# Running the body of a fused attention and token-mixing kernel as 64-row products

## The chip, the cores and the metric

The kernel runs on one core of one Trainium2 chip. The time is that of one execution on the device, in microseconds (us). TensorE (PE) multiplies and writes to the PSUM banks; VectorE (DVE) and ScalarE (ACT) read PSUM, GpSimd (POOL) does not in this kernel; SyncE (SP) mostly issues DMAs.

## The reference

Two layers follow each other, for each of 8 batches, with a sequence of 3200 rows:

```python
B, S, D = 8, 3200, 256;  d_qk = d_hyper = 64
scores = (1.0 / S) * z @ z.T             # z: S x 64
attn   = np.maximum(scores, 0.0) ** 2
x      = u * (attn @ v)                  # u, v: S x 256
wq, wk = x @ w_q, x @ w_k                # S x 64
mixed  = (1.0 / np.sqrt(64)) * (wq @ wk.T) @ x
out    = np.maximum(mixed, 0.0) @ w_out
```

The second layer has no nonlinearity between its two products, so the kernel forms `wk.T @ x` (64 x 256, the "heads") first and multiplies `wq` by that (the "mix").

## The kernel before

**Tiling.** A batch's 3200 rows are 25 row tiles of 128, in seven groups: six of 512 rows and a last one of 128 (`LASTG`). A score tile is one row tile against one group. Since the scores are symmetric, a tile that lies near the diagonal is computed once and turned by a DMA transpose for its mirror image (`is_turned`, tiles `tt` and `ttl`). All tiles to be scored stand in one list, `tiles`, and are taken in pairs.

**A score pair** (`scores`, L209). `z` is held transposed and twice, in the upper and the lower 64 partitions (`zT2`), so the two products of a pair use 64 rows of the array each and go into the two banks of one PSUM slot. There are three such slots (`ps_tile`, pool `pps`). The slot is emptied with a ReLU (`first_stage`, L232 on DVE, L228 on ACT) into `g`, and `second_stage` squares it (L247 on POOL, L245 on ACT) into the fp16 tile `at`.

**The second product** (`second_product`, L287). For each of a group's four blocks of 128 rows and each of 25 row tiles, one product with all 128 rows and 256 columns adds to an accumulator. A group's accumulators fill two banks, `acc0` (blocks 0 and 1) and `acc1` (blocks 2 and 3). When a half is complete, `gate` (L313) multiplies it by `u` on DVE and writes `x`; `turn_x` transposes `x` by DMA.

**The second layer.** `projections` (L335) gives queries and keys, two products of 128 rows; `turn_keys` transposes the keys by DMA; `double_keys_queries` copies queries by DMA (L359) and keys on POOL (L360) into the other half; `heads` (L366) adds up `wk.T @ x` over the groups; `mix` (L414, 64-row products) and `proj` (L439, 128-row products) follow, with evictions on ACT (L426, L463) and a DMA of the result. The last group's mix and projection are squeezed into a slot of another step (`side_mix`, `side_proj`).

**The order** is written by hand as phases (the `while groups` loop). A phase scores up to six tiles, stages them, and then issues some 24 second products; a mix or a set of keys and heads goes into a phase when `mix_due` or `key_due` says so. Loads and turns are hung on phase numbers (`due`). A head (`first_pair`, `turn_first`) and a tail (`last_gram`, `last_heads`, and the last mixes and projections) are written out one by one.

Of the kernel before, what the change touches and what calls it, by code (L numbers as in the profile page):

```python
# [16 lines left out]
def kernel(  # L17
# [17 lines left out]
    ND = D // P  # L35
    W = 512
    widths = [512] * 6 + [128]
    starts = [sum(widths[:i]) for i in range(len(widths))]
    NG = len(widths)
    assert sum(widths) == S and dqk == 64 and dh == 64 and ND == 2  # L40

    LAG = 2
# [7 lines left out]
    NAT = 14  # L50

# [8 lines left out]
    pg = ctx.enter_context(tc.tile_pool(name="pg", bufs=8))  # L60
# [3 lines left out]
    pq = ctx.enter_context(tc.tile_pool(name="pq", bufs=9))  # L64
    prt = ctx.enter_context(tc.tile_pool(name="prt", bufs=3))
    pps = ctx.enter_context(tc.tile_pool(name="pps", bufs=3, space=bass.MemoryType.PSUM))
# [5 lines left out]
    def acc_tile(half, name, dtype=FP32):  # L72
        n = W if dtype == FP32 else 2 * W
        return pacc.tile([P, n], dtype, tag=f"acc{half}", name=name)
# [5 lines left out]
    def rows(t, b):  # L80
        return t[b].rearrange("(p n) d -> p n d", n=NT)

# [28 lines left out]
    def turn_first(c):  # L111
        n0, nn = ZCH[c]
        if c < 2:
            tp = acc_tile(c, "ztp", FP16)
# [12 lines left out]

    def load_z(b):
# [18 lines left out]

    wq32 = consts.tile([P, ND, dh], FP32, tag="wq32", name="wq32")
    wk32 = consts.tile([P, ND, dh], FP32, tag="wk32", name="wk32")
    wqk = consts.tile([P, ND, 2, dh], FP16, tag="wqk", name="wqk")  # L150
    wq2 = consts.tile([P, ND, 2, dh], FP16, tag="wq2", name="wq2")
# [4 lines left out]
    def load_weights():  # L156
        wo32[0] = px.tile([P, ND, D], FP32, tag="x_sb", name="wo32")
        nc.sync.dma_start(out=wq32[:], in_=moe_w_q.rearrange("(c p) h -> p c h", p=P))
        nc.sync.dma_start(out=wk32[:], in_=moe_w_k.rearrange("(c p) h -> p c h", p=P))
        nc.sync.dma_start(out=wo32[0][:], in_=moe_w_out.rearrange("(c p) e -> p c e", p=P))  # L160

    def cast_weights():
        nc.gpsimd.tensor_copy(out=wqk[:, :, 0, :], in_=wq32[:])
        nc.gpsimd.tensor_copy(out=wqk[:, :, 1, :], in_=wk32[:])
        for half in range(2):
            nc.gpsimd.tensor_copy(out=wq2[:, :, half, :], in_=wq32[:])
            nc.gpsimd.tensor_copy(out=wk2[:, :, half, :], in_=wk32[:])
        nc.gpsimd.tensor_copy(out=wo[:], in_=wo32[0][:])

    LASTG = NG - 1

# [5 lines left out]

    def rows_of(gi):
        return [starts[gi] // P + n for n in range(widths[gi] // P)]
# [16 lines left out]
    NTILE = len(tiles)  # L200
    made, turned = {}, {}

    def scores(p0):
        pair = tiles[p0 : p0 + 2]
        sc = ps_tile("sc")
        for h, (b, gi, ti) in enumerate(pair):
            gs, gw = starts[gi], widths[gi]
            half = h * dqk
            nc.tensor.matmul(  # L209
                out=sc[:, h, 0:gw],  # L210
                lhsT=zT[b][half : half + dqk, ts(ti, P)],
                rhs=zT[b][half : half + dqk, ds(gs, gw)],
# [5 lines left out]
    def pieces(p0):  # L218
        ws = [widths[gi] for _, gi, _ in tiles[p0 : p0 + 2]]
# [4 lines left out]
    def first_stage(p0, sc, on_act):  # L224
        g = pg.tile([P, 2, W], FP32, tag="g", name="g")
        for hs, w in pieces(p0):
# [11 lines left out]
    def second_stage(p0, g, on_act):  # L238
        at = pat.tile([P, 2 * W], FP16, tag="at", name="at")
        at0 = 0  # L240
        for hs, w in pieces(p0):
# [8 lines left out]
        for tile_ in tiles[p0 : p0 + 2]:  # L250
# [8 lines left out]
        for b, gi, gj, n0, nn, c0, c1 in blocks:  # L259
# [8 lines left out]
    accs = {}  # L268

    def weights(b, gi, ti, j):  # L270

# [6 lines left out]
    def second_product(b, gi, rows_, first, last):  # L278

        nj = widths[gi] // P  # L280
        halves = range((nj + 1) // 2)
        if first:
            for half in halves:
                accs[half] = acc_tile(half, f"acc{half}")

        def one(ti, j):
            nc.tensor.matmul(  # L287
                out=accs[j // 2][:, ds((j % 2) * D, D)],
                lhsT=weights(b, gi, ti, j),
                rhs=vs[b][:, ti, :],  # L290
                start=(first and ti == rows_[0] and j % 2 == 0),
                stop=(last and ti == rows_[-1] and (j % 2 == 1 or j == nj - 1)),
            )

        todo = []
        if last:
            for half in halves:
                for ti in rows_:
                    for j in range(2 * half, min(2 * half + 2, nj)):
                        todo.append(lambda ti=ti, j=j: one(ti, j))  # L300
                run = todo.pop()
                todo.append(lambda run=run, half=half: (run(), gate(b, gi, half)))
        else:
            for ti in rows_:
                for j in range(nj):
                    todo.append(lambda ti=ti, j=j: one(ti, j))
        return todo

    def gate(b, gi, half):
        if half == 0:  # L310
            xs[b, gi] = px.tile([P, 4, D], FP16, tag="x_sb", name="x_sb")
        n = min(2, widths[gi] // P - 2 * half)
        nc.vector.tensor_mul(  # L313
            out=xs[b, gi][:, 2 * half : 2 * half + n, :].rearrange("p n d -> p (n d)"),
            in0=accs[half][:, 0 : n * D],
            in1=us[b, gi][:, 2 * half : 2 * half + n, :].rearrange("p n d -> p (n d)"),
        )
        if 2 * half + n == widths[gi] // P:
            us.pop((b, gi))
            turn_x(b, gi)  # L320

    def turn_x(b, gi):
        nn = widths[gi] // P
        xTs[b, gi] = pxt.tile([P, 4, ND, P], FP16, tag="xT_sb", name="xT_sb")
        nc.sync.dma_start_transpose(
            out=xTs[b, gi][:, 0:nn, :, :].rearrange("p n a s -> p (n a) s"),
            in_=xs[b, gi][:, 0:nn, :].rearrange("p n d -> p (n d)"),
        )


    def projections(b, gi, w, out, start=True):

        gw = widths[gi]
        for ac in range(ND):
            nc.tensor.matmul(  # L335
                out=out,
                lhsT=w[:, ac, :, :].rearrange("p t h -> p (t h)"),
                rhs=xTs[b, gi][:, 0 : gw // P, ac, :],
                start=(start and ac == 0),
                stop=(ac == ND - 1),  # L340
            )

    def projections_out(b, gi, out):
        gw = widths[gi]
        qks[b, gi] = pq.tile([P, W], FP16, tag="qk", name="qk")
        nc.scalar.copy(out=qks[b, gi][:, 0:gw], in_=out)  # L346

    def turn_keys(b, gi):
        gw = widths[gi]
        ks[b, gi] = pk.tile([P, 4, 2, dh], FP16, tag="kx", name="kx")  # L350
        nc.sync.dma_start_transpose(
            out=ks[b, gi][:, 0 : gw // P, :, :].rearrange("p n a h -> p n (a h)"),
            in_=qks[b, gi][:, 0:gw],
        )

    def double_keys_queries(b, gi):
        gw = widths[gi]
        nn = gw // P
        nc.sync.dma_start(out=qks[b, gi][dh:P, 0:gw], in_=qks[b, gi][0:dh, 0:gw])  # L359
        nc.gpsimd.tensor_copy(out=ks[b, gi][:, 0:nn, 0, :], in_=ks[b, gi][:, 0:nn, 1, :])  # L360

    def heads(b, gis, ps, stop=True):

        parts = [(gi, n) for gi in gis for n in range(widths[gi] // P)]
        for gi, n in parts:
            nc.tensor.matmul(  # L366
                out=ps[:, 1, 0:D],
                lhsT=ks[b, gi][:, n, :, :].rearrange("p a h -> p (a h)"),
                rhs=xs[b, gi][:, n, :],
                start=((gi, n) == parts[0]),  # L370
                stop=(stop and (gi, n) == parts[-1]),
            )

    def heads_out(b, gis, ps):
        if gis[0] == 0:
            hacc[b] = psml.tile([P, D], FP32, tag="ha", name="ha")
            nc.vector.tensor_copy(out=hacc[b][:], in_=ps[:, 1, 0:D])
        elif gis[-1] < LASTG:
            nc.vector.tensor_add(out=hacc[b][:], in0=hacc[b][:], in1=ps[:, 1, 0:D])  # L379
        else:  # L380
            heads_done(b, ps[:, 1, 0:D])

    def heads_done(b, part):
        hss[b] = psml.tile([P, D], FP16, tag="hs", name="hs")
        nc.vector.tensor_add(out=hss[b][:], in0=hacc.pop(b)[:], in1=part)  # L385

    def last_gram(b, gi, ps):
        nj = widths[gi] // P
        for n in range(nj):
            for cc in range(ND):  # L390
                nc.tensor.matmul(
                    out=ps[:, ds(cc * D, D)],
                    lhsT=xs[b, gi][:, n, ds(cc * P, P)],
                    rhs=xs[b, gi][:, n, :],
                    start=(gi < LASTG and n == 0 and cc == 0),
# [402 lines left out]
```

## Time and profile before

| | |
|---|---|
| three timed runs | 820.94, 819.31, 819.62 us; median 819.62 |
| span of the profiled execution | 815.5 us |
| TensorE's mean granted clock | 0.997 |
| PE / DVE / ACT / POOL busy | 791.9 / 490.1 / 476.7 / 487.0 us |
| second products (L287) | 5000 instructions, 67% of the chain that ended last |
| scores (L209) | 920 instructions, 13% of the chain |
| DMA, mean of the span | 176 GB/s |

The profile is of one execution, and its span is from the first to the last instruction; the time of an execution is some 4 us more. Matmuls are pipelined and the ends of their records are modelled, so the pitch of a stream of products is read from start to start, and not from a record's duration.

### The profile page before, as it was taken

Reading aid. Unit: us, or ns where it says so; the run is one execution under the profiler, and the core shown is the slowest. Engines: PE = TensorE matmul, PEld = TensorE weight load, DVE = VectorE, ACT = ScalarE, POOL = GpSimd, SP = SyncE. Lnnn points to the kernel's source line nnn. Section 1 sums busy time; section 2 is a strip of 40 time slices with the busy share of each in tenths; the row PEclk is TensorE's granted clock in tenths of the full one; section 3 lists DMA queues with packets and bytes.
Section 4 is the critical chain, followed back from the end, with each engine's and each line's share of the span. In section 5 each row is a group of like instructions: output and inputs, shape, how many; then the busy total and the mean of one; then the engine's idle time right before and its main releaser. Section 6 shows DMA issues by size and latency. Waiting matters only on the chain.

```text
span 815.5 us, 16776 instructions
## 1 busy us (share of the span) xinstructions
PE 791.9 (97%) x6778; PEld 585.5 (72%) x6778; DVE 490.1 (60%) x515; ACT 476.7 (58%) x529; POOL 487.0 (60%) x352
## 2 busy tenths in 40 slices
PE   6899999999999999999999999999999989999995
PEld 3677777777777777777777777777777757767773
DVE  3756566556675566755666556755665546655524
ACT  4655556555665566656665656755675645565545
POOL 5976677555775647654576446854676446665510
PEclk9999999999999999999999999999999999999999
DMA  5999999997999959997999969999899995778436
GB/s 108 212 170 189 133 182 174 198 196 143 181 182 205 216 116 203 165 236 162 194 169 198 205 145 181 188 201 172 189 167 171 192 215 129 158 151 174 113 100 239
DMA packets 331389, 143.20 MB, mean 176 GB/s; under 512 B 307440, under 2 KB 313392, under 8 KB 331312
## 3 DMA queue, kind: packets, MB, share of 16 engines
q1 hardware_dynamic: 302752, 125.70, 74.7%
q0 software_dynamic: 28272, 15.98, 18.4%
q8 instruction: 53, 0.87, 0.5%
q10 hardware_dynamic: 288, 0.46, 0.2%
q14 instruction: 24, 0.20, 0.1%
HBM read 59.38 MB, written 26.21 MB: 105 GB/s over the span
## 4 chain that ended last, share of the span: by engine, by line
PE 93%; DMA 2%; issue 2%; DVE 1%; POOL 1%; ACT 1%; DVEq 0%; ACTq 0%; POOLq 0%
PE acc L287 67%; PE sc L209 13%; PE fo L439 5%; PE qk L366 3%; PE qk L335 3%; PE mx L414 2%; DMA v_sb<-in_v_dram 1%; POOL at L247 1%; DVE g L232 1%; ACT rt L426 1%; DVE x_sb L313 0%; DMA z<-in_z_dram 0%; DMA xT_sb<-x_sb 0%; PE ztp L118 0%; DVE zT L121 0%
## 5 line engine op out<-in xcount | busy, mean ns | idle before, releaser
L247 POOL TENSOR_TENSOR at<-g 128x1024 f16<-128x1024 f32 x235 | 432.5, 1852 | 246.5 <-DVE g L232 145.5
L232 DVE TENSOR_SCALAR g<-sc 128x1024 f32<-128x1024 f32 (+1 forms) x339 | 387.5, 1185 | 190.6 <-PE sc L209 173.4
L287 PE MATMUL acc<-v_sb,at 128*128 128x256 f16 x3656 | 448.6, 274 | 3.6 <-DMA v_sb<-in_v_dram 2.7
L287 PEld LDWEIGHTS <-at 128*128 128x128 f16 x3656 | 345.0, 98 | 113.7 <-issue 70.2
L228 ACT ACTIVATE g<-sc 128x1024 f32<-128x1024 f32 x129 | 132.0, 1023 | 205.4 <-PE sc L209 187.3
L245 ACT ACTIVATE at<-g 128x1024 f16<-128x1024 f32 (+2 forms) x233 | 236.1, 1029 | 0.1
L287 PE MATMUL acc<-v_sb,tt 128*128 128x256 f16 x1152 | 150.0, 274 | 0.0
L209 PE MATMUL sc<-zT 64*128 64x512 f16 x920 | 130.4, 381 | 2.4 <-DVE hs L385 0.9
L287 PEld LDWEIGHTS <-tt 128*128 128x128 f16 x1152 | 112.9, 98 | 13.3
L313 DVE TENSOR_TENSOR x_sb<-acc,u_sb 128x512 f16<-128x512 f32 (+1 forms) x104 | 69.3, 668 | 67.3 <-PE acc L287 62.9
L426 ACT ACTIVATE rt<-mx 128x1024 f16<-128x1024 f32 (+1 forms) x49 | 49.0, 1010 | 57.6 <-PE mx L414 56.9
L209 PEld LDWEIGHTS <-zT 64*128 64x128 f16 x920 | 35.2, 94 | 50.7 <-issue 30.0
L463 ACT ACTIVATE fo<-fo 128x1024 f32<-128x1024 f32 (+1 forms) x44 | 42.9, 976 | 27.5 <-PE fo L439 25.3
L439 PE MATMUL fo<-wo,rt 128*128 128x256 f16 x386 | 49.6, 273 | 4.3 <-ACT rt L426 4.3
L360 POOL COPY kx<-kx 128x256 f16<-128x256 f16 (+1 forms) x54 | 20.0, 376 | 49.5 <-DMA kx<-qk 49.5
L439 PEld LDWEIGHTS <-rt 128*128 128x128 f16 x386 | 37.1, 98 | 10.9 <-ACT rt L426 6.1
L346 ACT CAST qk<-qk 128x512 f16<-128x512 f32 (+1 forms) x54 | 28.7, 544 | 27.3 <-PE qk L366 12.2
L366 PE MATMUL qk<-x_sb,kx 128*128 128x256 f16 x191 | 28.4, 273 | 2.9 <-POOL kx L360 2.9
L379 DVE TENSOR_TENSOR ha<-ha,qk 128x256 f32<-128x256 f32 x31 | 13.1, 421 | 29.8 <-ACT qk L346 29.8
L366 PEld LDWEIGHTS <-kx 128*128 128x128 f16 x195 | 19.0, 98 | 15.2 <-POOL kx L360 3.4
L335 PE MATMUL qk<-xT_sb,wqk 128*128 128x512 f16 (+1 forms) x108 | 29.9, 358 | 0.0
L287 PE MATMUL acc<-v_sb,ttl 128*128 128x256 f16 x192 | 22.6, 273 | 0.0
(46 smaller groups left out, 146.0 us busy)
## 6 DMA issues: line engine op xcount, KB each, us to landing
u_sb<-in_u_dram SPq DMA_DIRECT2D x48, 512.0 KB, 5.0
out_dram<-fo SPq DMA_DIRECT2D x43, 512.0 KB, 3.9
v_sb<-in_v_dram POOLq DMA_DIRECT2D x35, 320.0 KB, 6.1
qk<-qk SPq DMA_DIRECT2D x47, 64.0 KB, 4.0
zd<-in_z_dram POOLq DMA_DIRECT2D x7, 400.0 KB, 7.4
tt<-at SPq DMA_TRANSPOSE x144, 4.4
out_dram<-fo SPq DMA_DIRECT2D x9, 256.0 KB, 2.9
u_sb<-in_u_dram SPq DMA_DIRECT2D x8, 128.0 KB, 2.9
```

The lines of the kernel that those rows point to most:

```text
L209: nc.tensor.matmul(out=sc[:, h, 0:gw], lhsT=zT[b][half : half + dqk, ts(ti, P)], rhs=zT[b][half : half + dqk, ds(gs, gw)], start=True, sto ...
L228: nc.scalar.activation(out=g[:, hs, 0:w], in_=sc[:, hs, 0:w], func=RELU, scale=GSCALE)
L232: nc.vector.tensor_scalar(out=g[:, hs, 0:w], in0=sc[:, hs, 0:w], scalar1=0.0, scalar2=GSCALE, op0=AOP.max, op1=AOP.mult,)
L245: nc.scalar.square(out=out, in_=g[:, hs, 0:w])
L247: nc.gpsimd.tensor_mul(out=out, in0=g[:, hs, 0:w], in1=g[:, hs, 0:w])
L287: nc.tensor.matmul(out=accs[j // 2][:, ds((j % 2) * D, D)], lhsT=weights(b, gi, ti, j), rhs=vs[b][:, ti, :], start=(first and ti == rows_[ ...
L313: nc.vector.tensor_mul(out=xs[b, gi][:, 2 * half : 2 * half + n, :].rearrange("p n d -> p (n d)"), in0=accs[half][:, 0 : n * D], in1=us[b, ...
L335: nc.tensor.matmul(out=out, lhsT=w[:, ac, :, :].rearrange("p t h -> p (t h)"), rhs=xTs[b, gi][:, 0 : gw // P, ac, :], start=(start and ac ...
L366: nc.tensor.matmul(out=ps[:, 1, 0:D], lhsT=ks[b, gi][:, n, :, :].rearrange("p a h -> p (a h)"), rhs=xs[b, gi][:, n, :], start=((gi, n) == ...
L426: nc.scalar.activation(out=rts[b, gi][:, :, 0:gw], in_=ps[:, :, 0:gw], func=RELU)
L439: nc.tensor.matmul(out=banks[jf // 2][:, ds((j - jf) * D, D)], lhsT=rt[:, dc, ts(j, P)], rhs=wo[:, dc, :], start=(dc == 0 and j == jf), st ...
L463: nc.scalar.mul(out=flat_out[:, sl], in_=part, mul=FINAL_SCALE)
```

## The change

All products of the loop but the output projections become pairs of 64-row products, one on the upper 64 partitions and one on the lower.

- *Second product*: for each block and row tile there are two products, one per half of the rows; each half has accumulators of its own, so there are four accumulator banks (`acc00`, `acc01`, `acc10`, `acc11`), and the score slots are two (`pps` has `bufs=2`).
- *Gate*: ACT copies the upper accumulator into an SBUF tile `both`, DVE adds the lower one, POOL multiplies by `u`. `x` is laid out so that its transpose has blocks 0 and 1 in the upper and blocks 2 and 3 in the lower partitions; that is what 64-row projections and mixes read. The copy of queries by DMA is gone.
- *Heads*: partial sums of the upper and lower rows stay apart (`hacc` is twice as wide) and are added when the batch is complete.
- *z* of the next batch is loaded densely and copied twice by DVE; before, it was loaded with gaps and copied once.
- *The side products* are gone: the last group has a mix and a projection like the others.
- *The order* comes from a small planner that runs when the kernel is built. It keeps a clock for each of four engines, adds the weight of every step, and takes next, at PE's clock, an extra (keys, mix, projection), a score pair or a step of the second product, with `lead = 95` steps of scoring ahead. Score evictions and squares go to the engine whose clock would end first. Two ready projections are issued one after the other.

```diff
-    pg = ctx.enter_context(tc.tile_pool(name="pg", bufs=8))
+    pg = ctx.enter_context(tc.tile_pool(name="pg", bufs=7))
+    psum = ctx.enter_context(tc.tile_pool(name="psum", bufs=3))
...
-    pps = ctx.enter_context(tc.tile_pool(name="pps", bufs=3, space=bass.MemoryType.PSUM))
+    pps = ctx.enter_context(tc.tile_pool(name="pps", bufs=2, space=bass.MemoryType.PSUM))
...
     def load_z(b):
+        zdense[b] = pz.tile([P, NT, dqk], FP16, tag="zn", name="zn")
+        nc.gpsimd.dma_start(out=zdense[b][:], in_=rows(z, b))
+
+    def double_z(b):
         zds[b] = pz.tile([P, NT, 2, dqk], FP16, tag="zd", name="zd")
-        nc.gpsimd.dma_start(out=zds[b][:, :, 0, :], in_=rows(z, b))
-
-    def double_z(b):
-        nc.vector.tensor_copy(out=zds[b][:, :, 1, :], in_=zds[b][:, :, 0, :])
+        for half in range(2):
+            nc.vector.tensor_copy(out=zds[b][:, :, half, :], in_=zdense[b][:])
...
+        def one(j, r):
+            if first and j == js[0]:
+                accs[half, r] = acc_tile(half, r, f"acc{half}{r}")
             nc.tensor.matmul(
-                out=accs[j // 2][:, ds((j % 2) * D, D)],
-                lhsT=weights(b, gi, ti, j),
-                rhs=vs[b][:, ti, :],
...
+                out=accs[half, r][:, ds((j % 2) * D, D)],
+                lhsT=weights(b, gi, ti, j)[top(r), :],
+                rhs=vs[b][top(r), ti, :],
+                start=(first and j == js[0]),
+                stop=(last and j == js[-1]),
             )
...
+        return [lambda j=j: [one(j, r) for r in range(2)] for j in js]
...
     def gate(b, gi, half):
...
-        nc.vector.tensor_mul(
-            out=xs[b, gi][:, 2 * half : 2 * half + n, :].rearrange("p n d -> p (n d)"),
-            in0=accs[half][:, 0 : n * D],
-            in1=us[b, gi][:, 2 * half : 2 * half + n, :].rearrange("p n d -> p (n d)"),
+        both = psum.tile([P, 2 * D], FP32, tag="both", name="both")
+        nc.scalar.copy(out=both[:, 0 : n * D], in_=accs[half, 0][:, 0 : n * D])
+        nc.vector.tensor_add(
+            out=both[:, 0 : n * D], in0=accs[half, 1][:, 0 : n * D], in1=both[:, 0 : n * D]
         )
+        for r in [half] if widths[gi] == W else range(2):
+            nc.gpsimd.tensor_mul(
+                out=xs[b, gi][:, 0:n, :, r, :].rearrange("p n c d -> p (n c) d"),
...
+    def use_pair():
+        open_slot()
+        p = produced[0]
+        produced[0] += 1
+        sc = scores(p)
+        clock[PE] += 0.22
+        held = []
+        done = evict(
+            clock[PE] + HOP, 1.19, 1.03, lambda on_act: held.append(first_stage(p, sc, on_act))
+        )
+        slots.append(done)
+        pending.append((done, p, held[0]))
...
+    def half_done(b, gi, half):
+        ready = clock[PE] + HOP
+        t = give(ACT, ready, 0.58)
+        t = give(DVE, t, 0.7)
+        free_at[half] = t
+        t = give(POOL, t, 0.97)
+        gate(b, gi, half)
...
+    def acc_step():
+        if not work and not open_rows():
+            return False
+        fn, (b, gi, half), begins, closes, row = work.pop(0)
+        if begins:
+            clock[PE] = max(clock[PE], free_at.get(half, 0.0))
+        fn()
+        clock[PE] += 0.1093
+        used.add(row)
+        if closes:
+            half_done(b, gi, half)
+        return True
...
+        if room and extra and (not wanted or turn_about[0]):
+            turn_about[0] = False
+            extras.remove(extra)
+            extra[2]()
+            if extra[1] == "proj":
+                more = [x for x in extras if x[1] == "proj" and x[0] <= clock[PE]]
+                for x in more[:1]:
+                    extras.remove(x)
+                    x[2]()
+        elif room and wanted:
+            turn_about[0] = True
+            use_pair()
+        elif acc_step():
+            done_acc += 1
```

More of the change, by code (lines that the diff above doesn't have):

```diff
@@ new lines, with give, at_time, flush @@
+    PE, DVE, ACT, POOL = range(4)
+    clock = [0.0] * 4
+    HOP = 0.15
+    def give(engine, ready, weight):
+        clock[engine] = max(clock[engine], ready) + weight
+        return clock[engine] + HOP
+    slots = [0.0, 0.0]
+    free_at = {}
+    row_at = {}
+    pending, later, extras, blocks = [], [], [], {}
+    def at_time(t, fn):
+        later.append((t, fn))
+    def flush():
+        now = clock[PE]
+        while True:
+            ripe = [x for x in later if x[0] <= now]
+            if not ripe:
+                break
+            x = min(ripe, key=lambda x: x[0])
+            later.remove(x)
+            x[1]()
@@ L570, in first_pair @@
-    def first_pair(p0, on_act):
-        second_stage(p0, first_stage(p0, scores(p0), on_act), on_act)
+        fn()
+        for half in range(2)
+        for ti in rows_
+        for fn in second_product(0, 0, half, ti, first and ti == rows_[0], False)
+    ]
+    def first_pair(p, on_act):
+        for turn in second_stage(p, first_stage(p, scores(p), on_act), on_act):
+            turn()
     make_identity(nc, ident)
@@ new lines, with mixed @@
+    while extras or later:
+        if later:
+            x = min(later, key=lambda x: x[0])
+            later.remove(x)
+            x[1]()
+        else:
+            extras.pop(0)[2]()
+    assert not pending and len(keyed) == 1
+    def mixed(b, gi):
+        ps = ps_tile("mx")
+        mix(b, gi, ps)
+        mix_out(b, gi, ps)
+    hb, hgi = keyed.pop()
+    psh = ps_tile("hd")
+    heads(hb, hgi, psh)
+    psg = acc_tile(1, 0, "xtx")
+    last_gram(last, LASTG - 1, psg)
+    heads_out(hb, hgi, psh)
```

763 lines of the change are left out of this document (381 added, 382 removed).

## The prediction

> **What bounds the kernel now.** I read the page first (busy times, chain), then the timeline of TensorE, then the groups with their shapes kept apart.
>
> ```profile
> PE 791.9 (97%) x6778; PEld 585.5 (72%) x6778; DVE 490.1 (60%) x515; ACT 476.7 (58%) x529; POOL 487.0 (60%) x352
> PE 93%; DMA 2%; issue 2%; DVE 1%; POOL 1%; ACT 1%; DVEq 0%; ACTq 0%; POOLq 0%
> ```
>
> TensorE is busy for 97% of the span and carries 93% of the chain. The other engines stand at 58 to 60%, so only what PE does or waits for can move the end. The timeline of PE around 224 us, and one long run of products near the end, show what PE's time is made of:
>
> ```profile
> 221.94 0.28 PE L335 MATMUL qk<-xT_sb,wqk 128*128 128x128 f16 x2
> 222.05 1.69 PE L287 MATMUL acc<-v_sb,at 128*128 128x256 f16 x14
> 223.68 0.82 PE L209 MATMUL sc<-zT 64*128 64x512 f16 x6
> 224.43 2.79 PE L287 MATMUL acc<-v_sb,at 128*128 128x256 f16 x24
> 227.16 0.82 PE L209 MATMUL sc<-zT 64*128 64x512 f16 x6
> 227.91 2.79 PE L287 MATMUL acc<-v_sb,at 128*128 128x256 f16 x24
> ...
> 777.35 3.89 PE L287 MATMUL acc<-v_sb,at 128*128 128x256 f16 x34
> 781.07 0.59 PE L335 MATMUL qk<-xT_sb,wqk 128*128 128x512 f16 x2
> ```
>
> 34 full products before another full product take 781.07 - 777.35 = 3.72, or 0.1094 each. 24 of them before scores take 227.16 - 224.43 = 2.73, where 24 x 0.1094 = 2.63: the change to 64-row products costs 0.10. Six scores take 227.91 - 227.16 = 0.75 with a change back. The two products of a pair run at once (a single one would need 512/256 x 0.107 = 0.214, and six in a row 1.28), so three pairs are 0.65 and the change back is 0.10 again. A round trip costs 0.20.
>
> ```profile
> 206.60 0.82 PE L209 MATMUL sc<-zT 64*128 64x512 f16 x6
> ...
> 207.10 2.36 DVE L232 TENSOR_SCALAR g<-sc 128x1024 f32<-128x1024 f32 x2 [1.85 <-PE sc L209]
> ...
> 207.31 1.02 ACT L228 ACTIVATE g<-sc 128x1024 f32<-128x1024 f32 x1
> ```
>
> The first pair streams until 206.60 + 0.22, the second until 207.03; their evictions start 0.28 later on either engine. In the tail ACT's rt, from 799.22 for 1.02, releases a product at 800.30: 0.06 back. From ACT to DVE it is 0.04 (an ACT cast at 209.52 for 0.58, then DVE at 210.14). I use 0.28 out and 0.07 back, and these means: score eviction 1.219 on DVE (L232), 1.023 on ACT (L228); square 1.049 on ACT, 1.892 on POOL; 512-wide eviction 0.585 on ACT (L346), 512-wide sum or product 0.689 on DVE (L313), 256-wide 0.383 (L504) and 0.424 (L313).
>
> **What is removed.** Counted in the built orders of PE's instructions, the row mode changes 176 times each way before and 35 after; only the output projections, the first transposes and the last Gram product stay at 128 rows. 141 round trips x 0.20 = -28.2. The span without it would be 787. PE's wait of 3 us at 660 for keys that POOL was still copying (the heads are now taken only once that copy is placed well ahead) may go too: -3 (0 to -3).
>
> **What costs PE nothing.** 5000 full products become 5000 pairs; if a pair of 256 columns streams in the 0.109 of one full product, the sum is the same. Projections, heads and mixes also keep their streamed columns. The side products of the last group (14 x 0.056 + 14 x 0.109 = 2.3) turn into 14 projections and some small pairs, about the same. The 54 copies qk<-qk on SP's queue and the 128-byte pieces of z go: the core's DMA is lighter, but PE waits for DMA some 3 us in all, at the start, so I give it nothing.
>
> The pair's pitch is the one assumption that the trace shows only at 512 columns. From above: 0.003 us more per pair (three scoring pairs in 0.65 are 0.217 each, against 0.214 streamed) is 5500 x 0.003 = +16. From below, nothing: 256 columns take 0.107 anyhow. I take 0.
>
> PE also issues twice as many instructions, four per pair. Eight transposes of 128 columns at 17.60 lead to scores at 18.14: 0.54, less 0.10 for the change, is 0.055 for each load and product, so four instructions fit into 0.110. The Trainium skill, in "TensorE: Matmul & The Clock Gate", section "Wait — 56ns, not 53.3ns?", says that without hardware decode the sequencer spends about 62 ns on each product; two per pair would be 0.124 in place of 0.109, an estimated +80 us on the sum below. The trace's 0.055 does not agree with that rule.
>
> **What is added on the other engines.** Each of 104 gates becomes an ACT copy, a DVE sum and one or two POOL products. DVE: 390 x 1.219 + 96 x 0.689 + 45 sums of heads at 0.689 + 14 copies of z at 1.096 + some 10 = about 600. ACT: 216 x 1.049 + 96 x 0.585 + 62 x 1.023 + 48 x 1.023 + 47 x 0.585 + 40 x 1.023 + 10 = about 475. POOL: 236 x 1.892 + 96 x 1.039 + 50 = about 600. None bounds by its sum. But score slots fall from three to two, and an accumulator half comes free only after ACT and then DVE. I went through the built order of two middle batches, laying each eviction behind the instruction ahead of it in its engine's order. Four places make PE wait:
>
> (a) *Turn of a batch.* The last group has one half; its last product is followed at once by the first of the next group into the same banks. Floor, with idle engines: 0.28 + 0.38 + 0.04 + 0.42 + 0.07 = 1.19. ACT has a square or a score in hand there: 1.7 and 2.0 in the two batches. 7 turns x 1.6 = +11 (8 to 14). Before, scores stood between.
>
> (b) *A closing chunk of four rows* (the second group of nearly every batch). The half is needed again after 8 pairs, 0.87, and is free after 0.28 + 0.585 + 0.04 + 0.689 + 0.07 = 1.67: 0.8. Right behind its sum DVE has the two copies of z, 2.2 us, ahead of the other half's sum and the next scores: another 0.9. Before, one copy of 1.1 lay behind three slots. 7 x 1.7, plus early closings of the first batch 2 and the last batch 0.8: +15 (8 to 20).
>
> (c) *Two projections in a row.* The second takes the slot of the pair scored just before the first: 0.28 + 1.22 + 0.07 = 1.57 against 0.98 of first projection and change, 0.6 short. It grows where a sum for a half stands ahead of that eviction in DVE's order and its ACT copy stands behind squares and rt: one case, counted from the end of the mix before it: square to 0.65, rt to 1.67, copy to 2.26, sum to 2.99, score eviction to 4.21, and the second projection, due at 2.94, starts at 4.29. Seven such places gave 1.35, 1.35, 0.95, 0.2, 1.5, 0.7 and 0. 20 places x 0.85 = +17 (8 to 30).
>
> (d) Scores after such a place, and mixes, wait 0.05 to 0.2 here and there: +4 (0 to 10).
>
> Ordinary closings have 2.2 to 2.6 of other work against 1.67 and pass; quiet scoring reuses a slot after 2.6 against 1.57 and passes.
>
> **Head and tail.** In the head the third score waits for one of two slots, under 0.5. In the tail the last gate is longer by an ACT copy and POOL products, about 1.5, while a group costs ACT 1.02 + 0.60 = 1.62 where two groups took 802.20 - 798.71 = 3.49 before. +1 (-2 to +4).
>
> **Sum.** 815.5 - 28.2 - 3 + 11 + 15 + 17 + 4 + 1 = 832.3 of span. The three runs have a median of 819.62, 4.1 above the profiled span; the same 4.1 gives 836.4. I predict 836.
>
> **Rivals.**
> *The engines stand idle when gates and projections come (faster).* Then (a) to (c) are at their floors, 7 x 1.19 = 8, 7 x 0.8 + 2 + 0.8 = 8, and 13 of the 20 places (those with no other work between) x 0.6 = 8, (d) is 0, and the span is 815.5 - 28.2 - 3 + 24 + 1 = 809, the time 813. For it: no engine is above 75%, and PE's own waits let queues drain. Against it: the squares and z copies named above. It decides where waits per batch fall below 4.2 us (about 30 in all). Chance 0.14, with part of "same".
> *The pair is a few ns slower than one full product.* 5500 x 0.003: 852. No row has a pair of 256 columns. Chance 0.1.
> *Pairs are bound by issue.* The 0.54 for eight, taken with no change in it, is 0.0675 per load and product, 0.135 per pair: 5500 x 0.026 = +143, about 975 with the waits partly covered. The 0.055 speaks against it. The section of the Trainium skill cited above is a rule of this kind. Chance 0.04.
> *The change doesn't do what it says.* Two products that add to two banks at once may not overlap; the scoring pairs that do overlap start afresh each time. 5000 x 0.109 = +546, about 1365. Nothing in the profile speaks for it. Chance 0.03.
>
> **How the numbers follow.** My own case has 0.69; its time, 836, is the prediction. The range, 813 to 857, reaches from the idle-engine rival to the slower pair. Under 0.2%, 1.6 us, a measurement cannot tell the two apart: faster 0.13, same 0.04, slower 0.83.
>
> **What would show it.** Right: 70 changes of mode at 0.10; PE's idle time, some 45 us more than now, released by DVE sums at the first product of a group and by DVE or ACT evictions ahead of the second of two projections; 34 pairs in 3.72. Wrong: a pair pitch that is not 0.109, or PE without idle time in the middle batches, which would give about 790.

## The result and the profile after

The changed kernel takes 879.02 us (median of 4 runs, 876.65 to 880.78), the kernel before 819.46 beside it: a ratio of 1.073 (95% interval 1.070 to 1.076). The forecast was 836, in a range of 813 to 857: the sign was right, the size was not. The profiled executions have spans of 877.4 and 815.5, so 61.9 us have to be explained. The ratios here and below leave out executions that lie more than 1.5% above the fastest of the same kernel; three of the experiments have one such execution among their four.

The page after, the line of busy times and that of the chain by engine:

```profile
PE 793.1 (90%) x12373; PEld 689.3 (79%) x12373; DVE 602.3 (69%) x601; ACT 465.1 (53%) x558; POOL 642.0 (73%) x527
...
PE 15%; ACT 2%; DVE 2%; issue 1%; POOL 1%; DMA 1%; POOLq 0%; SPq 0%; ACTq 0%; DVEq 0%
```

The shares of the chain add up to some 22% of the span: it breaks off on its way back, so it shows only the end here. PE is busy as long as before and idle for 84 us where it was idle for 24. DVE came to 602 (forecast 600) and ACT to 465 (475); POOL came to 642, 42 more than forecast. A piece of PE's timeline without a wait:

```profile
330.50 0.47 PE L216 MATMUL sc<-zT 64*128 64x512 f16 x2
330.71 1.45 PE L295 MATMUL acc<-v_sb,at 64*128 64x256 f16 x22
331.91 0.47 PE L216 MATMUL sc<-zT 64*128 64x512 f16 x2
```

22 products, 11 pairs, take 331.91 - 330.71 = 1.20, so 0.109 a pair, and there is no extra time where scores and second products meet. This part did what was forecast. The idle time is in the list of what PE waited for (total us, times, longest):

```profile
PE qk L389 <- POOL kx L382: 21.3, 10, 5.2
PE fo L439 <- DVE g L239: 8.2, 12, 0.9
PE hd L389 <- POOL kx L382: 6.7, 1, 6.7
PE acc L295 <- ACT both L310: 6.0, 8, 1.0
PE qk L353 <- ACT fo L464: 5.2, 3, 2.3
...
PE acc L295 <- DVE both L311: 4.0, 14, 0.5
PE mx L416 <- DVE g L239: 3.2, 6, 0.7
```

Before, the only entry for the keys was this:

```profile
PE qk L366 <- POOL kx L360: 2.9, 1, 2.9
```

I expected even that one to go. Here is the worst of the ten places after, first on PE's timeline, then the way of those keys on the other engines:

```profile
137.84 0.38 PE L353 MATMUL qk<-xT_sb,wqk 64*128 64x128 f16 x4
143.45 1.03 PE L389 MATMUL qk<-x_sb,kx 64*128 64x256 f16 x8 [5.23 <-POOL kx L382]
```

```profile
128.53 0.58 ACT L365 CAST qk<-qk 128x512 f16<-128x512 f32 x1
...
129.84 2.65 SPq L336 DMA_TRANSPOSE xT_sb<-x_sb  x1
...
132.59 2.14 SPq L370 DMA_TRANSPOSE kx<-qk  x1
...
143.11 0.52 POOL L382 COPY kx<-kx 128x128 f16<-128x128 f16 x2 [5.28 <-DMA kx<-qk]
```

The keys are evicted at 129.11. Their transpose is issued 3.5 later, behind another transpose in SP's queue, and lands 10.5 after that; POOL stands at the copy for 5.28 until it does, and PE until 143.45. The next keys step, which multiplies these keys, was due at 137.84, nine us after the eviction. The planner allows 8 us.

The wait costs more than itself. Windows of the same trace (length, then busy us and count of PE, PEld, DVE, ACT, POOL, then the granted clock, DMA share, GB/s):

```profile
100.00:138.00 38.00, 36.31 (x607) 32.29 (x603) 29.62 (x29) 19.06 (x23) 32.94 (x27) 1.00 0.96 158
138.00:150.00 12.00, 6.77 (x71) 4.40 (x69) 5.18 (x7) 3.63 (x6) 4.29 (x5) 0.72 0.74 106
150.00:244.00 94.00, 90.06 (x1450) 78.63 (x1448) 68.20 (x67) 52.23 (x61) 78.07 (x62) 1.00 0.89 169
244.00:256.00 12.00, 8.42 (x101) 6.19 (x98) 6.89 (x9) 4.36 (x6) 5.94 (x6) 0.72 0.91 171
```

The granted clock is 1.00 elsewhere and 0.72 around the two waits. The trace's clock records show half rate for 6.8 us from 142.1 and from 247.9, and for 3.4 us from 459.5 and 568.8: each follows one of the four idle stretches of 3.5 to 5.2 us in the body. Stretches of 2.28 (at 521), 1.58 and 1.69 us are followed by none. (In the head, where PE stops often, 3.4 us at half rate follow a stop of 2.4.)

**The ledger.** For every product I took the time to the next start beyond its pitch (the starts in these traces lie 0.056, 0.109 and 0.216 us apart for 128, 256 and 512 columns; half of that for one of a pair, 0.10 more at a change of row mode) and put it down to the wait that the trace shows there, to half rate, or to the rest. The body runs from 25 us to the last second product, the closing part from there.

| us | before | after | difference |
|---|---|---|---|
| body: products at their pitch, mode changes | 756.7 | 729.1 | -27.6 |
| body: waits for the keys | 3.1 | 23.9 | +20.8 |
| body: all other waits | 2.6 | 48.8 | +46.2 |
| body: products at half rate | 1.6 | 10.2 | +8.6 |
| body: rest | 2.5 | 3.6 | +1.1 |
| head | 24.9 | 25.0 | +0.1 |
| closing part | 24.1 | 36.9 | +12.8 |

In the closing part, 6.9 of the 36.9 are a wait for the last keys and 3.4 are half rate. The cut at 25 us is fixed, so the head's row can't show a later head: at the cut the changed kernel is seven second products and three score pairs behind, an estimated 1.4 us by the pitches above, which then stand in the body's first row.

### The profile page after: what moved, and what is told of

Same layout as the page of the kernel before. It is cut to its first block, busy times and chain, and to the rows that moved or that the text cites. A ratio compares the mean times of both kernels' runs of the same rounds, so it can differ in the third digit from the quotient of the medians.

```text
span 877.4 us, 28408 instructions
## 1 busy us (share of the span) xinstructions
PE 793.1 (90%) x12373; PEld 689.3 (79%) x12373; DVE 602.3 (69%) x601; ACT 465.1 (53%) x558; POOL 642.0 (73%) x527
## 3 DMA queue, kind: packets, MB, share of 16 engines
q0 software_dynamic: 6768, 15.98, 12.8%
## 5 line engine op out<-in xcount | busy, mean ns | idle before, releaser
L239 DVE TENSOR_SCALAR g<-sc 128x1024 f32<-128x1024 f32 (+2 forms) x402 | 478.3, 1199 | 112.3 <-PE sc L216 99.6
L254 POOL TENSOR_TENSOR at<-g 128x1024 f16<-128x1024 f32 (+1 forms) x250 | 455.2, 1828 | 114.4 <-DVE g L239 90.0
L295 PE MATMUL acc<-v_sb,at 64*128 64x256 f16 x7312 | 521.0, 272 | 17.8 <-ACT both L310 6.0
L295 PEld LDWEIGHTS <-at 64*128 64x128 f16 x7312 | 416.8, 95 | 62.0 <-issue 22.1
L252 ACT ACTIVATE at<-g 128x1024 f16<-128x1024 f32 (+1 forms) x218 | 228.9, 1054 | 190.7 <-DVE g L239 187.1
L216 PE MATMUL sc<-zT 64*128 64x512 f16 x920 | 196.4, 382 | 4.5 <-DVE g L239 1.8
L295 PE MATMUL acc<-v_sb,tt 64*128 64x256 f16 x2304 | 182.7, 270 | 0.0
L315 POOL TENSOR_TENSOR x_sb<-both,u_sb 128x512 f16<-128x512 f32 (+1 forms) x112 | 133.3, 1194 | 62.9 <-DVE both L311 61.7
L295 PEld LDWEIGHTS <-tt 64*128 64x128 f16 x2304 | 130.6, 94 | 12.6 <-issue 0.6
L311 DVE TENSOR_TENSOR both<-acc,both 128x512 f32<-128x512 f32 (+1 forms) x104 | 69.4, 668 | 51.0 <-ACT both L310 46.5
L464 ACT ACTIVATE fo<-fo 128x1024 f32<-128x1024 f32 (+2 forms) x54 | 47.6, 890 | 40.5 <-PE fo L439 28.9
L439 PE MATMUL fo<-wo,rt 128*128 128x256 f16 x400 | 53.4, 278 | 12.8 <-DVE g L239 8.2
L389 PE MATMUL qk<-x_sb,kx 64*128 64x256 f16 x382 | 32.4, 279 | 21.5 <-POOL kx L382 21.3
L382 POOL COPY kx<-kx 128x128 f16<-128x128 f16 (+1 forms) x101 | 26.3, 289 | 26.6 <-DMA kx<-qk 26.5
```

The costliest lines, as they stand in the source:

```text
L216: nc.tensor.matmul(out=sc[:, h, 0:gw], lhsT=zT[b][top(h), ts(ti, P)], rhs=zT[b][top(h), ds(gs, gw)], start=True, stop=True,)
L239: nc.vector.tensor_scalar(out=g[:, hs, 0:w], in0=sc[:, hs, 0:w], scalar1=0.0, scalar2=GSCALE, op0=AOP.max, op1=AOP.mult,)
L252: nc.scalar.square(out=out, in_=g[:, hs, 0:w])
L254: nc.gpsimd.tensor_mul(out=out, in0=g[:, hs, 0:w], in1=g[:, hs, 0:w])
L295: nc.tensor.matmul(out=accs[half, r][:, ds((j % 2) * D, D)], lhsT=weights(b, gi, ti, j)[top(r), :], rhs=vs[b][top(r), ti, :], start=(first ...
L311: nc.vector.tensor_add(out=both[:, 0 : n * D], in0=accs[half, 1][:, 0 : n * D], in1=both[:, 0 : n * D])
```

## The experiments

Before took 818.9 to 820.5 in these comparisons.

**The keys' copy later.** The planner's allowance for one group of each batch, the one with the worst waits, rises from 8 to 14 us.

```diff
-        at_time(done + 8.0, lambda: double_keys(b, gi))
+        at_time(done + (14.0 if gi == LASTG - 1 and b < last else 8.0), lambda: double_keys(b, gi))
```

> The planner's allowance between the eviction of a group's keys and the POOL copy of them is 14 us in place of 8 for the sixth group of each batch but the last (the heads of that group move with it); nothing else is changed by hand. Theory A (late keys): at five batch turns PE stands 1.7 to 5.2 us at the heads because the turned keys land 10 to 14 us after their eviction, and the granted clock falls to half for 3.4 to 6.8 us after each. Then PE's idle time at L389 in the body falls from 21.5 us to under 6, the half-clock stretches between 140 and 670 us (20 us) are gone, and the time falls by 21 + 8 to about 848 us (842 to 855). Theory B (slots and banks cost more than I put down, and would take the waits over): under 8 us fall, 871 to 879.

Measured: 897.67, ratio 1.095 (1.091 to 1.099). A miss.

```profile
PE qk L389 <- POOL kx L382: 30.4, 18, 4.1
```

The heads are put right behind the copy, wherever it stands. A later copy does not make the keys come sooner; it moved the heads, and lateness spread from 10 places to 18. POOL's own wait for the keys' transposes fell from 26.5 to 6.0 us at the same time, so a POOL that isn't held is no gain by itself.

**Projections one at a time.** The block that issues a second ready projection (`if extra[1] == "proj": ...`) is gone.

> Two ready projections are no longer issued one after the other; 20 more changes of mode each way. Theory A: the waits at the second of two projections (L439 for DVE, and L353, L416 behind them: 18 us of idle time and 0.17 of pipeline for each) go for the most part, -16, and the 20 round trips cost +4; the late keys stay. About 867 us (860 to 874). Theory B (the slots are what binds, wherever the projections stand): the waits move to the scores, and the time is within 3 us of 879 or above.

Measured: 871.6, ratio 1.062 (1.060 to 1.065). The wait of 8.2 for score evictions ahead of a second projection is gone from the list, for 110 mode changes in place of 70. Term (c) is real; the run gains 7.4 in all, net of these changes.

**z as before.** `z` is loaded with gaps and copied once by DVE.

> z of the next batch is loaded with gaps and copied once, as in the kernel before. The prediction's term (b) gave the second copy on DVE about 0.9 us per batch, 6 in all: about 873 us (870 to 877). If the 128-byte pieces make the keys land later, as a rival has it (the z load's DMA stands beside the late keys), the idle time at L389 grows by some us and the time is 879 or more. If the dense z load itself holds the keys up, idle time at L389 falls under 15 and the time is under 870.

Measured: 883.01 (874.94 to 890.98), ratio 1.072 (1.065 to 1.079). No gain; the copies of z, a part of term (b), had no price that shows, though a spread of 16 us could hide much of the 6 expected.

**A score pair in the place of a blocked bank.**

```diff
+        elif (
+            room and (work or open_rows()) and work[0][2] and free_at.get(work[0][1][2], 0.0) > now + 0.2
+            and p < NPAIR and (p < NAT or all_used(p - NAT))
+        ):
+            use_pair()
         elif acc_step():
```

> Where the next step of the second product would wait more than 0.2 us for its accumulator, the planner takes a score pair first if a slot is free. Prediction's terms (a) and (b) put 1.2 to 2.0 us at each turn and 0.8 at each short closing: if these sizes hold, -5 to -8, about 873 us. The trace of the changed kernel shows only 10 us of idle time for ACT's and DVE's work on accumulators (25 waits), so if those are the whole of it, -2 to -4 and 876 us.

Measured: 872.98 (866.14 to 877.75), ratio 1.064 (1.057 to 1.071). The waits for ACT's copies fell from 6.0 to 4.8, those for DVE's sums rose from 4.0 to 7.3: the banks' waits as a whole did not fall. What fell is the wait for the keys (21.3 to 14.7) and with it the half rate (10.2 to 3.0); I put that down to the shifted order, which nothing here shows by itself.

**Heads two keys steps later.**

```diff
-        prior = keyed.pop(0) if keyed else None
+        prior = keyed.pop(0) if len(keyed) >= 2 else None
...
-                if x[0] <= now and (x[1] != "keys" or not keyed or keyed[0] in doubled)
+                if x[0] <= now and (x[1] != "keys" or len(keyed) < 2 or keyed[0] in doubled)
```

> The heads of a group are multiplied two keys steps after its keys instead of one (17 to 33 us later instead of 9 to 19), nothing else; one more buffer for x, paid for by loading w_q and w_k into such a buffer. Theory A (the keys come late because one step, 9 to 19 us, is about as long as their way over the SP queue, the transposing DMA and POOL's copy, 12 to 14 us, and each such wait brings half-clock stretches): the 21.5 us behind POOL's copies in the body go to under 3, their drain (12 x 0.17 = 2 us) and most of the body's half clock (about 9 us) with them: 879 - 32 = 847, range 839 to 857. Theory B (PE waits for POOL because POOL and the queues fall behind the order's clocks, so that every later place is met by a later copy, as one run suggests in which the copy was placed 6 us later and the time rose): the waits come back at other places, 868 or more. Theory C (the waits alone count, the half clock comes from elsewhere): 855 to 860.

Measured: 863.54, ratio 1.055 (1.049 to 1.061), in none of the three ranges. In the body PE no longer waits for keys at all, and half rate there is 1.7 us. Both went, 32.4 us by the ledger, but the span fell by 17.7:

```profile
PE acc L296 <- DVE both L312: 11.4, 24, 1.3
PE acc L296 <- POOL at L255: 7.6, 7, 2.5
PE fo L440 <- DVE g L240: 7.4, 12, 0.8
```

The other waits rose from 48.8 to 65.0, at DVE's sums (4.0 to 11.4) and POOL's squares (3.1 to 7.6) above all. While PE stood for the keys, the other engines had, as I read it, caught up. The half rate went with the long waits: theory C, which kept it, is out, and A is half right.

**Key transposes on ACT's queue** (`nc.scalar.dma_start_transpose` in `turn_keys`).

> The transposing DMA of the keys is issued on ACT's queue, right behind ACT's eviction of them, instead of SP's, where it stood 3 to 6 us behind transposes and loads that were waiting themselves. Theory A (the wait in SP's queue makes the keys late): the waits behind POOL's copies fall from 21.5 us to 5 to 10 and the half clock by some 8 us; ACT pays about 1 us for each of 54 issues, beside other work: 858, range 850 to 868. Rival (the landing, 5 to 10 us behind other loads, makes them late): the waits stay at 17 us or more, 872 to 885.

Measured: 1102.73, ratio 1.344 (1.338 to 1.349). Neither theory. ACT's timeline:

```profile
155.01 0.59 ACT L365 CAST qk<-qk 128x512 f16<-128x512 f32 x1
162.86 1.21 ACTq L370 DMA_TRANSPOSE kx<-qk  x1
164.12 1.02 ACT L235 ACTIVATE g<-sc 128x1024 f32<-128x1024 f32 x1 [8.52 <-issue]
```

The transpose sits behind a semaphore wait in ACT's own order, here for 7.3 us and up to 11.6, and every eviction behind it waits too. Once issued it lands in 2.3 us (median). The trace does not name whose semaphore it is, but here it lets go 0.3 us after the last transpose that SP had issued has landed (162.56), and 51 of the 54 transposes on ACT's queue are issued within 0.5 us of such a landing. The Trainium skill, "DMA: Bandwidth & Descriptors", section "Silent corruption: two transposing streams in flight at once", says that a second stream's transposes must wait until the first's have completed; the run agrees with that, as no transpose of ACT's is in flight together with one of SP's. So in this program a second queue does not shorten the way of the keys: a transpose stands behind all others.

**The closing part in another order.** The products `xtx` and two mixes stand ahead of the heads of the last keys.

> In the closing part only: the products of the last two groups (xtx) and two mixes are put ahead of the heads of the last keys, which waited 6.7 us for POOL's copy and were followed by 3.4 us at half clock. Theory (the closing part is 13 us longer than before because of this wait and of what the half clock makes of the steps behind it): the part shrinks from 36.9 to about 28 us: 870, range 866 to 874. Rival (the closing part is bound by the last evictions and stores): 876 to 881.

Measured: 874.62, ratio 1.067 (1.062 to 1.073). The wait for the last keys fell from 6.7 to 2.6, but the closing part only from 36.9 to 35.9 (mean clock 0.79 in it), so the theory, which had 28, fails.

**Four edits together**: heads two steps later, single projections, pairs at blocked banks, and the closing part reordered.

> Together: heads two keys steps later, closing part reordered, no second of two output projections in a row, a score pair in the place of a wait for a bank. If the four lists of waits are apart from each other: 879 - 32 (keys) - 7.5 (projections) - 6 (pairs) - 8 (closing part) = 825.5, range 815 to 840, so about the kernel before (819) and not clearly below it. If the waits are one another's cause (POOL, ACT and the queues late as a whole): 850 or more.

Measured: 857.84 (849.91 to 871.45), ratio 1.042 (1.035 to 1.049), little better than the heads alone. POOL's waits, and the squares that PE then lacked (its profiled execution took 871 us, 14 above the median):

```profile
POOL kx L383 <- DMA kx<-qk: 49.3, 13, 8.1
```

```profile
PE acc L296 <- POOL at L255: 21.4, 12, 4.0
```

**The copy later still** (16 in place of 8 us), on top of the four. With two steps of slack the heads needn't wait for it.

> As the run with all four edits, and POOL's copy of the keys is placed 16 instead of 8 us after their eviction; with the heads two keys steps later it still comes in time. In that run POOL waited 49 us for the keys' transposes in 13 or so places and PE 21 us for POOL's squares. Theory (POOL, held at a copy whose DMA has not landed, keeps the squares and gates behind it, and PE meets these late): POOL's wait for the keys' DMA falls under 10 us, PE's for the squares under 6, and the time from 858 to 843, range 833 to 850. Rival (POOL is late because it is busy, 642 us of 870): 855 or more.

Measured: 846.74, ratio 1.028 (1.020 to 1.036). The theory's signs came: POOL's wait is down to 4.0, PE's for squares is gone from the list, and the time is in the range. How many of the 11 us come of it is open, since the waits of the run before are those of its 871 us, and the same edit without the other three brought only 2 (below).

```profile
POOL kx L383 <- DMA kx<-qk: 4.0, 1, 4.0
```

**Second products with 128 rows again**, in the order of the change.

```diff
-                accs[half, r] = acc_tile(half, r, f"acc{half}{r}")
+                accs[half, 0] = acc_tile(half, 0, f"acc{half}0")
...
-                lhsT=weights(b, gi, ti, j)[top(r), :],
-                rhs=vs[b][top(r), ti, :],
+                lhsT=weights(b, gi, ti, j),
+                rhs=vs[b][:, ti, :],
```

> The accumulation alone goes back to 128-row products in one bank for each half (the gate takes ACT's copy of it, DVE's sum is gone), while the order of the change stays, in which score pairs are put in one at a time: mode changes rise from 70 to 1070. Theory A (a mode change costs 0.10 us, whatever the order): +100 us on PE, less the 10 to 20 us of waits that a slower PE and a DVE with 69 us less to do no longer meet: 965, range 955 to 980. Rival (a change costs nothing while the loads run ahead; the saving was not there): 860 to 875.

Measured: 927.04, ratio 1.126 (1.119 to 1.133). With 0.10 booked for each of 1000 more changes, the products rose by 98.3, and only 5.6 of the rest are left over: a change costs 0.10 to 0.11. But the time rose only by 48, less than either part of theory A allowed, since waits and half rate fell by 53.6 (table below). With a PE that is slower throughout, and a DVE without the sums, the same chains on the other engines are in time.

**Without DVE's sum.** The gate takes the upper rows alone.

> DVE's sum of the two accumulators is left out (the gate takes the upper rows' part alone), 104 instructions of 0.67 us; PE's products and order are the same. Theory A (DVE with its 69 us of sums is behind the order's clocks, and the waits of PE for DVE, 19 us in the body, come of that): they fall to about 7, and the banks open 0.8 us sooner: 866, range 860 to 871. Rival (the late keys alone set the body's waits, DVE's are their echo): 874 to 880.

Measured: 860.45, ratio 1.046 (1.039 to 1.053): 18.6 less for 69 us less on DVE. The time is at the lower end of theory A's range, but only a third of it went A's way. In the body:

```profile
PE qk L386 <- POOL kx L379: 15.5, 10, 4.4
...
PE mx L413 <- DVE g L239: 4.1, 7, 0.7
...
PE fo L436 <- DVE g L239: 3.5, 9, 0.4
```

All waits of PE for DVE fell from 18.8 to 10.3 (7 were expected). In the ledger, all waits but those for keys fell by 6 us, those for the keys by another 6, and half rate from 10.2 to 4.7. So DVE's sums may have a part in the late keys too. That part is not shown: the run with another closing part has the same order in the body, and its wait for the keys there was 17.2 us in place of 21.3, so some 4 us differ from one execution to the next.

**Without POOL's copy of the keys.** The heads multiply what the transpose leaves.

> POOL's doubling of the keys is left out (the heads multiply what the transpose leaves, 101 copies of 0.29 us gone), the order is the same. PE then waits for the transposing DMA itself. Theory (the DMA's way is what is late): the 21.5 us fall only by the copies' own part, 0.5 to 1 us for each of 12, and POOL, no longer held 26 us, gives its squares sooner: 868, range 862 to 874. Rival (POOL's order makes the keys late): they fall under 8 us and the half clock with them: 850 to 858.

Measured: 866.55 (860.52 to 875.95), ratio 1.051 (1.042 to 1.059).

```profile
PE qk L390 <- DMA kx<-qk: 5.4, 3, 3.0
```

The copies' own time is 0.3 each, but the wait for keys in the body fell by 16. So POOL's place in the chain was a cause of late keys, and not only the last link. The way that I see for it, argued from the order of SP's queue and not shown by itself: held at a copy, POOL is late with its gates, SP's transposes of these stand at the head of SP's queue, and the next keys' transpose stands behind them. For the keys of each batch's sixth group, where the long waits were, the time from eviction to landing did fall, from 10.9 us in the mean of seven to 8.9; over all 54 transposes it didn't (6.8 and 7.1). These are the rival's waits in the theory's time: the other waits rose by 9.6 again.

**Heads and copy later**, without the other edits.

> The kernel with the heads two keys steps later, and POOL's copy 16 instead of 8 us after the eviction of the keys, nothing else. Theory (POOL, held at a copy whose DMA has not landed, delays the squares and gates behind it, SP's transposes of these wait in turn, and the next keys stand behind them in SP's queue; both edits together open this ring): PE waits for POOL's squares fall from 7.6 to under 2, POOL's wait for the keys from 26 to under 6, and the time from 863.5 to 852, range 846 to 857; the keys' whole price in the change is then 27 us. Rival (without PE's late keys POOL is simply busy): 860 to 866.

Measured: 861.62, ratio 1.051 (1.047 to 1.055). POOL waits 2.2 us for keys and the squares' wait is gone, yet only 2 us come of it; the rival holds. The keys' whole price in the change is some 17 us, not 27.

**The best version**: the four edits, the later copy, v of the second batch loaded 18 us sooner, and the last heads put behind the first closing projection.

> As the run with all four edits and the later copy, and two more: the loads of the second batch's v are placed 18 us earlier (PE waited 4.8 us for the last of them, and 6.8 us at half clock followed), and the heads of the last two groups are put behind the first output projection of the closing part (PE waited 3.5 us for the last keys, and 10 us at half clock followed). Theory: 846.7 - 4.8 - 3.4 - 3.5 - 4 = 831, range 826 to 838; still above the kernel before by what the banks' handover and the longer closing part cost. Rival (the closing part is bound by the chain from the last keys to the last stores): 838 to 845.

Measured: 838.98 (838.14 to 839.76), ratio 1.023 (1.020 to 1.026): the best of them, and still slower than before. The wait for v at the turn to the second batch is gone; one at 32 us, right behind the head, which the run before it had too (3.5), takes 4.3. The closing part fell to 31.3. The time lies just outside the theory's range and in the rival's. So no version at or below the kernel before was found.

The ledger for the runs that carry the argument (profiled executions):

| us | after | heads later | no POOL copy | 128 rows | four, copy later | best |
|---|---|---|---|---|---|---|
| products, changes | 729.1 | 729.3 | 729.2 | 827.4 | 731.0 | 731.3 |
| waits for keys | 23.9 | 0 | 6.0 | 1.5 | 3.2 | 3.2 |
| other waits | 48.8 | 65.0 | 58.4 | 25.8 | 43.3 | 40.5 |
| half rate | 10.2 | 1.7 | 3.3 | 2.0 | 5.1 | 2.7 |
| rest | 3.6 | 3.6 | 3.1 | 9.2 | 4.5 | 4.0 |
| head | 25.0 | 25.0 | 24.0 | 25.0 | 25.0 | 24.9 |
| closing part | 36.9 | 35.1 | 34.4 | 35.4 | 34.7 | 31.3 |
| span | 877.4 | 859.7 | 858.4 | 926.3 | 846.8 | 838.0 |

## Why the prediction was right or wrong

*Removed, -28.2.* Right: 70 mode changes, and -27.6 in the body's products. The run with 128 rows prices a change at 0.10 once more.

*Pitch of a pair, issue, overlap.* Right: 0.109 a pair. The rivals of a slower pair, of issue and of missing overlap fall.

*Terms (a) to (d), +47.* The sum came out, +46.2, but partly by luck: (a) and (b) were 8 too high, (d) 8 too low, and once PE doesn't wait for keys the same waits are 65.0. (a) ACT's copies hold PE for 6.0 in 8 places, 1.03 at the longest; with what a stop adds beyond the records' modelled ends (0.17 each) and the lower bank's 0.2 behind some of them this is the floor, 8 in place of 11. (b) The copies of z cost nothing that shows, and PE waits for DVE's sums only 4.0 in 14 places; with (a) and POOL's squares it comes to 18 against 26. (c) 8.2 in 12 places behind DVE's evictions, 5.2 in three where a keys step follows a projection, and with smaller ones and the 0.17 of each some 19 against 17. (d) holds the remaining 12 against 4.

*The wait for keys, -3.* This step failed, and it began with a misread wait. I took the stop at 660 for a copy that POOL was still making; POOL stood idle there for its longest wait, 9.6 us, until the keys' transpose landed, and the copy itself took 0.39:

```profile
POOL kx L360 <- DMA kx<-qk: 49.5, 16, 9.6
```

So the way over the queue was long before the change too (up to 15.7 us from eviction to landing, and 13.9 after), and cost PE 2.9 only, because the heads came late enough. I had read "the heads are taken only once that copy is placed well ahead" as a guard, but it guards the place in the order, not the landing. Before, the keys of the last two groups went together, and from the keys' eviction to the time when their heads were due it was 10 to 25 us (less only twice, in the last batch). After, each group has a step, with 9 to 19 us between, and only 9 behind the sixth group of every batch, against a way of 12 to 14 in the four worst places (eviction, SP's queue, DMA, copy). I walked the built order with the durations of engines, and gave the queue and the DMA none. It became +20.8, and +8.6 of half rate behind it.

*Head and tail, +1.* Failed as well, +12.8: 6.9 for the last keys, the same way once more, 3.4 of half rate, the rest small.

*The clock* had no term at all. It was there to be read: before, 3.4 us at half rate follow PE's one stop of 2.9 us, at 664; I took the mean of 0.997 and looked no further.

*The size.* The three failed steps miss 23.8 + 8.6 + 11.9 = 44 us, the forecast missed 43. Taking them out gives back less: the keys 17 of 29 us. The waits are not apart from each other, and a sum of terms, each with its full price, holds for what is there, not for what a repair brings. The other waits of the best version, 40.5 us, were not taken apart further: what two score slots in place of three cost, no run shows.

## What to carry to other kernels

Where an order is drawn up by engine clocks, the queues need clocks too (not tried here): the way from an eviction over a DMA queue to the consumer has to fit into the shortest distance between two steps, not into a mean. An instruction that waits for a DMA on an in-order engine holds whatever is behind it, and if that feeds the queue that the DMA stands in, lateness can breed lateness (the ring as a whole was argued here, not shown); put it where the data has landed and let the consumer come a step later. Here the later consumer alone brought 15.5 us, the later copy with it 2 more, or 11 in the order with all four edits. A stop of PE of some 3 us or more is charged twice, so a few long waits are to be mended before many short ones.

## What was not expected of the hardware

*Half rate.* After the stops of 2.9 us and more in the body, before and after, PE's granted clock was 0.5 for 3.4 or 6.8 us. The Trainium skill, "TensorE: Matmul & The Clock Gate", section "HAM oscillation — how this bites in real kernels", warns of idle gaps over about 3.4 us; here 2.9 sufficed. Over all sixteen traces from 25 us on, each of the 74 stops of 2.9 us or more that began at full rate was followed by half rate, and 27 of the 56 between 1.5 and 2.9. The length of the stop doesn't decide alone. In each trace the clock changes only at multiples of 3.41 us from its first change. Cut at these, 98 stretches at full rate have PE's records in less than 40% of their time, and all are followed by a stretch at half rate; 3655 have them in more than 60%, and none is; of the 71 between, 18 are. So it matters how a stop falls on these boundaries: one of 2.53 us cost nothing in the run without POOL's copy. Eight products of 256 columns in the closing part then take 1.82 (849.27 to 851.09), with a change of mode behind them, in place of 0.98.

*Upper and lower rows out of step.* The two products of a pair need not run side by side:

```profile
312.56 0.40 PE L216 MATMUL sc<-zT 64*128 64x128 f16 x2
312.62 1.43 PE L295 MATMUL acc<-v_sb,at 64*128 64x256 f16 x21
313.82 0.38 PE L216 MATMUL sc<-zT 64*128 64x512 f16 x1
313.89 0.27 PE L295 MATMUL acc<-v_sb,at 64*128 64x256 f16 x1
314.00 0.38 PE L216 MATMUL sc<-zT 64*128 64x512 f16 x1
```

The upper score starts at 313.82, the lower at 314.00, and between them the lower half of the second product that stands ahead of both. The lag begins at 312.56 with a pair of unequal scores, 128 columns (a tile of the last group) for the upper rows and 512 for the lower: the upper rows go on 0.06 us later, the lower 0.22. It lasts until PE's next stop, at 325.8; the pitch stays 0.109.

*Transposes of two queues* were never in flight together in the run on ACT's queue (54 there, 255 on SP's), because ACT stood at semaphores of the program; no run shows what the queues do without them.
